# Older block's scores over the masked half: one turn for two blocks of attention weights

## The chip, the cores and the metric

The kernel runs on one core of a Trainium2 chip, so a run has one span. Time is device microseconds of that core; the runs of the kernel before took 629.08, 629.01 and 627.39 us, median 629.01. TensorE (PE) multiplies and turns matrices into PSUM; VectorE (DVE) and ScalarE (ACT) work on SBUF and PSUM; GpSimd (POOL) on SBUF; SyncE (SP) issues DMAs here. Engines run in order, each through its own list.

## The reference

Three layers follow each other: windowed attention with sinks, a gated product, and a mixture of experts with balanced routing. Only the attention is touched.

```python
batch, n_heads, seq, head_dim = (2, 8, 768, 64);  n_sink, window = (4, 128)
scores = (1 / sqrt(D)) * q @ k.T
keep = (pos[None, :] < n_sink) | ((rel >= 0) & (rel < window))     # rel = row - column
scores = where(keep, scores, -1e9);  a = exp(scores - max);  a /= sum(a) + 1e-9
return a @ v
```

A block of 128 queries sees its own block of 128 keys (lower triangle and diagonal), the older block before it (rel = 128 + row - column < 128: strictly the upper triangle), and the sinks. So for a window of up to 128 each pair of row and column is kept in at most one of the two blocks. Afterwards `x @ w_a * (x @ w_b) @ w_out` and the experts read the result.

## The kernel before

Attention is cut into 24 steps: 2 batches x 3 groups `g` of 256 queries (blocks `j` = 0, 1) x 4 pairs of heads `hp` (heads `h` = 0, 1). `attention` (L377) runs them as a software pipeline: iteration n (from -2 to 24) works on step n+2 (`turned`, L231), n+1 (`scores`, L257), n (`norm`: `factors`, `normed`, `sinks`; then `weights_turned` and `sinks_turned`) and n-1 (`copied`, `values`, `values_low`). The order of instructions on PE, ACT, DVE and POOL is the order of the code, written out by hand (`manual_schedule`, L595); SP's is planned.

In one iteration the order is: `norm` for step n, `copied` for n-1, `turned` for n+2, block 0's scores for n+1, `turned_low`, `values` and `values_low` for n-1, block 1's scores for n+1, then the turns of step n's weights and sinks. `fill` (L390) puts other PE work between them at seven places: dummy products up to iteration 8, and from iteration 9 on up to six products a time of the next stage (`early`, L460). From iteration 7 to 14 it also converts four raw weights (`word_steps`, L505: ACT, then DVE L518 to L525; the low part L541 on POOL), each over two iterations, the first of them the one that loads DVE (7, 9, 11, 13), the second POOL.

`scores` multiplies 128 queries with 264 columns for g > 0: the older block in columns 0 to 127, 8 sinks in 128 to 135, the own block in 136 to 263 (`KB` = 136). One DVE instruction (L277, shown as CUSTOM_DVE_ANT_0) adds the mask, scales, and keeps the row's extreme in `negmax`; ACT's exponential (L279) writes the weights `A2` and their `sums` (a second instruction reads the sum out). `factors` (L287, L288) makes 1/sum as `rs` on DVE; `normed` (L301) multiplies the weights by it on POOL, four instructions of 2 x 128 columns; `sinks` (L309 to L317) treats the sink columns on POOL. `weights_turned` (L334) turns up to 8 squares of 128 x 128 on PE: 2 blocks x 2 heads x (older, own). `copied` moves them to SBUF, head 0 on ACT (L349), head 1 on DVE (L347), the sinks on ACT (L343). `values` (L357, L367) multiplies with v.

Iterations 0 to 3 and 12 to 15 turn weights of g = 0 (no older block for block 0, so 6 squares, no sinks part); 4 to 11 and 16 to 23 have g > 0 and 8 squares. Scores run one iteration ahead: those of g > 0 stand in iterations 3 to 10 and 15 to 22.

PSUM has 8 buffers of 2 KB: 1 for turns of q and k, `SB` = 2 for scores, `ATB` = 3 for turned weights, 1 for values, 1 for the early products.

Of the kernel before, what the change touches and what calls it, by code (L numbers as in the profile page):

```python
# [9 lines left out]
F32 = mybir.dt.float32  # L10
F32R = mybir.dt.float32r
BF = mybir.dt.bfloat16
F16 = mybir.dt.float16
I32 = mybir.dt.int32
AF = mybir.ActivationFunctionType
# [35 lines left out]
         8: (("w", 3),), 9: (("v", 3), ("s", 1), ("q", 4), ("k", 4)), 13: (("v", 4), ("q", 5), ("k", 5)), 14: (("v", 5),)}  # L51
CONV_AT = (7, 9, 11, 13)
CONV_ON = (0, 0, 0, 0, 1)
SB, ATB = 2, 3
SINK = 8
WB, AB, NB, FB = 4, 2, 1, 2
KB = 128 + SINK
# [6 lines left out]
def f32(ap):  # L64
    return ap.bitcast(F32)


class Kernel:
# [17 lines left out]
    def constants(self, ctx, ge, att):  # L86
        nc, tc = self.nc, self.tc
        self.consts = c = ctx.enter_context(tc.tile_pool(name="consts", bufs=1))
        self.gep = ge.enter_context(tc.tile_pool(name="ge", bufs=1))
        m = att.enter_context(tc.tile_pool(name="masks", bufs=1))  # L90
        self.idle = m.tile([128, 512], BF, name="idle")
        nc.vector.memset(self.idle, 0.0)
        with tc.tile_pool(name="setup", bufs=1, side="right") as sp:
            rel = sp.tile([128, 128], F32, name="rel")
            nc.gpsimd.iota(rel, pattern=[[-1, 128]], base=0, channel_multiplier=1,
                           allow_small_or_imprecise_dtypes=True)
            self.ident = c.tile([128, 128], F32, name="ident")
            nc.vector.tensor_scalar(self.ident, rel, 0.0, None, op0=OP.is_equal)
            self.identr = m.tile([128, 128], F32R, name="identr")
            nc.vector.tensor_copy(self.identr, self.ident)  # L100
            raw = sp.tile([128, 2, 2], I32, name="raw")
            for i, s in enumerate((self.n_sink, self.window)):
                flat = bass.AP(tensor=s.tensor, offset=0, ap=[[1, 1]]).bitcast(I32)
                nc.gpsimd.dma_start(raw[:, i, :], bass.AP(tensor=flat.tensor, offset=0, ap=[[0, 128], [1, 2]]))
            col = sp.tile([128, 128], F32, name="col")
            nc.gpsimd.iota(col, pattern=[[1, 128]], base=0, channel_multiplier=0,
                           allow_small_or_imprecise_dtypes=True)
            low = sp.tile([128, 128], F32, name="low")
            nc.vector.tensor_scalar(low, rel, 0.0, None, op0=OP.is_ge)
            rel1 = sp.tile([128, 128], F32, name="rel1")  # L110
            nc.gpsimd.tensor_scalar(rel1, rel, 128.0, 1.0, op0=OP.add, op1=OP.mult)
            val = sp.tile([128, 2, 2], F32, name="val")
            nc.vector.tensor_copy(val, raw)
            neg = sp.tile([128, 2, 1], F32, name="neg")
            nc.vector.scalar_tensor_tensor(neg, val[:, :, 0:1], 0.0, val[:, :, 1:2], op0=OP.is_lt, op1=OP.add)
            sw = self.sw = c.tile([128, 2], F32, name="sw")
            nc.vector.scalar_tensor_tensor(sw, neg[:, :, 0], 4294967296.0, val[:, :, 0], op0=OP.mult, op1=OP.add)
            ns, win = sw[:, 0:1], sw[:, 1:2]

            def bias(eng, dst, keep):  # L120
                eng.tensor_scalar(dst, keep, BIG, -BIG, op0=OP.mult, op1=OP.add)

            snk = sp.tile([128, 128], F32, name="snk")
            nc.vector.tensor_scalar(snk, col, ns, None, op0=OP.is_lt)
            own = sp.tile([128, 128], F32, name="own")
            nc.vector.scalar_tensor_tensor(own, rel, win, low, op0=OP.is_lt, op1=OP.mult)
            own0 = sp.tile([128, 128], F32, name="own0")
            nc.vector.tensor_max(own0, own, snk)
            self.mask0 = m.tile([128, 128], F32, name="mask0")
            bias(nc.vector, self.mask0, own0)  # L130
            prev = sp.tile([128, 128], F32, name="prev")
            nc.vector.tensor_scalar(prev, rel1, win, None, op0=OP.is_lt)
            prev0 = sp.tile([128, 128], F32, name="prev0")
            nc.vector.tensor_max(prev0, prev, snk)
            self.mask1 = m.tile([128, 256 + SINK], F32, name="mask1")
            nc.gpsimd.memset(self.mask1[:, 128:KB], -BIG)
            bias(nc.gpsimd, self.mask1[:, KB:], own)
            bias(nc.gpsimd, self.mask1[:, 0:128], prev0)
            self.mask2 = m.tile([128, 256 + SINK], F32, name="mask2")
            bias(nc.gpsimd, self.mask2[:, 0:128], prev)  # L140
            bias(nc.gpsimd, self.mask2[:, 128:KB], snk[:, 0:SINK])
            bias(nc.gpsimd, self.mask2[:, KB:], own)
        self.negmax = c.tile([128, self.B * 6 * self.H], F32, name="negmax")
        self.sums = m.tile([128, self.B * 6 * self.H], F32, name="sums")

# [111 lines left out]
    def scores(self, st, j):  # L257
        nc, b, g, hp = self.nc, st.b, st.g, st.hp
        i = 2 * g + j
        if j == 0:  # L260
            st.A2 = self.aw.tile([128, 2, 2, 256 + SINK], F32, name="A", tag="A", bufs=4)
            st.r2 = self.aw.tile([128, 2, 2], F32, name="rs", tag="rs", bufs=4)
        T = self.T[b, hp]
        flat = T.rearrange("p t k c -> p t (k c)")
        c0 = KB if i == 0 else 0
        lo, n = (0, 128) if i == 0 else (KB * (i - 1), 256 + SINK)
        mask = self.mask0 if i == 0 else self.mask1 if i == 1 else self.mask2
        col0 = ((b * 6 + i) * self.H) + 2 * hp
        for h in range(2):
            s = self.atps.tile([128, 256 + SINK], F32, name="s", tag="s", bufs=SB)  # L270
            hs = slice(64 * h, 64 * h + 64)
            for t, (tq, tk) in enumerate(((0, 0), (0, 1), (1, 0))):
                nc.tensor.matmul(s[:, :n], T[hs, tq, 6 + i % 2, 0:128], flat[hs, tk, lo:lo + n],  # L273
                                 start=(t == 0), stop=(t == 2))
            sm = self.aw.tile([128, 256 + SINK], F32, name="sm", tag="sm", bufs=4)
            cc = slice(col0 + h, col0 + h + 1)
            nc.vector.tensor_tensor_reduce(out=sm[:, :n], in0=s[:, :n], in1=mask, scale=-self.scale, scalar=BIG,  # L277
                                           op0=OP.add, op1=OP.min, accum_out=self.negmax[:, cc])
            nc.scalar.activation(st.A2[:, j, h, c0:], sm[:, :n], AF.Exp, bias=self.negmax[:, cc], scale=-1.0,  # L279
                                 accum_out=self.sums[:, cc])  # L280

    def factors(self, st):
        nc = self.nc
# [6 lines left out]
    def normed(self, st):  # L290

        nc = self.nc
        i0 = 2 * st.g
        for h in range(2):
            for j in range(2):
                A = st.A2[:, j]
                blocks = A[:, h, KB if i0 + j == 0 else 0:]
                if i0 + j > 1:
                    blocks = bass.AP(tensor=A.tensor, offset=A.offset + h * (256 + SINK),
                                     ap=[list(A.ap[0]), [KB, 2], [1, 128]])  # L300
                nc.gpsimd.tensor_scalar(blocks, blocks, st.r2[:, j, h:h + 1], 1.0, op0=OP.mult, op1=OP.mult)  # L301

    def sinks(self, st):
# [15 lines left out]
    def sinks_turned(self, st):  # L319
# [3 lines left out]
        pt = self.atps.tile([128, 2, 128], F32R, name="pt", tag="at", bufs=ATB)  # L323
        for n in range(2):
            nc.tensor.transpose(pt[:, n, :], st.AS[:, n], self.identr)
        st.ps.append((pt[0:6 * SINK], None))

    def weights_turned(self, st, h):
        nc = self.nc
        pa = self.atps.tile([128, 4, 128], F32, name="pa", tag="at", bufs=ATB)  # L330
        a0 = 0 if st.g else 1
        for a in range(a0, 4):
            cols = slice(0, 128) if a % 2 == 0 else slice(KB, KB + 128)
            nc.tensor.transpose(pa[:, a, :], st.A2[:, a // 2, h, cols], self.ident)  # L334
        st.ps.append((pa, a0))

    def copied(self, st):

        nc = self.nc
        for n, (pa, a0) in enumerate(st.ps):  # L340
            if n == 2:
                st.ast = self.aw.tile([6 * SINK, 2, 128], F32R, name="ast", tag="ast", bufs=2)
                nc.scalar.activation(st.ast, f32(pa), AF.Copy)  # L343
                continue
            at = self.aw.tile([128, 4, 128], F32, name="at", tag="atb", bufs=4)
            if n:
                nc.vector.tensor_copy(at[:, a0:], pa[:, a0:])  # L347
            else:
                nc.scalar.activation(at[:, a0:], pa[:, a0:], AF.Copy)  # L349
            st.AT.append(at)  # L350

    def values(self, st):
        nc, D, b, g, hp = self.nc, self.D, st.b, st.g, st.hp
# [1000 lines left out]
```

## Time and profile before

| | |
|---|---|
| median of 3 runs | 629.01 us (627.39 to 629.08) |
| profiled execution | 627.7 us, of which the span 625.6 us |
| busy over the span | PE 97%, DVE 64%, ACT 54%, POOL 29% |
| granted TensorE clock | 0.9 or more of full speed in all but the last of 40 slices, 0.996 in the mean |
| attention | about 4.8 us to 130 us of the span |
| turned weights (L334) | 176 squares, 272 ns one in the median, 26.4 us of PE together |
| ScalarE's table loads | one, at the start; Exp, Copy, Abs, Sign and Relu all run later |

Busy time counts an instruction from start to end; matmuls overlap, so a busy PE can still have gaps between starts. In a time line a row's first number is its start, the second the time to its end. The first turn of q and k of an iteration (L237) tells where it begins: iteration 4 at 27.0 us, 6 at 35.7, 7 at 40.1, 9 at 50.2, 12 at 67.0, 16 at 86.5, 19 at 102.5, 20 at 107.9.

### The profile page before, as it was taken

What the parts mean: (1) busy time and instruction counts of PE and PEld (TensorE: products, weight loads), DVE (VectorE), ACT (ScalarE), POOL (GpSimd) and SP (SyncE); (2) the same over time, 40 slices, a digit from 0 to 9 for tenths busy, and PEclk for the clock granted to TensorE, in tenths of its full rate; (3) what the DMA queues carried; (4) which work ended last, traced back from release to release, by engine and by line L of the source; (5) the groups of instructions that cost most, each with busy time, mean ns of one, the idle gap of its engine ahead of it and who ended that gap; (6) DMA issues with size and microseconds to landing.
All of it is one profiled execution on the core that took longest, in us unless ns stands there. A gap on an engine that the chain in (4) does not pass through costs nothing.

```text
span 625.6 us, 10135 instructions
## 1 busy us (share of the span) xinstructions
PE 608.3 (97%) x3645; PEld 477.0 (76%) x3645; DVE 403.3 (64%) x864; ACT 339.0 (54%) x672; POOL 178.5 (29%) x300
## 2 busy tenths in 40 slices
PE   7999999999999999999999999999999999999994
PEld 5667777778877887777867766777788898888882
DVE  6788876669985766442114566656436878778781
ACT  4888777634552434213125566664436766667660
POOL 5657565410000000001024443434441322122221
PEclk9999999999999999999999999999999999999998
DMA  7977320025451433200031000000087788877841
GB/s 159 211 151 163 68 69 2 2 74 170 162 156 47 134 101 104 67 1 0 1 100 52 18 36 18 17 18 35 35 273 234 253 272 260 262 240 226 268 130 30
DMA packets 82602, 72.16 MB, mean 115 GB/s; under 512 B 41072, under 2 KB 69744, under 8 KB 82544
## 3 DMA queue, kind: packets, MB, share of 16 engines
q1 hardware_dynamic: 78704, 61.99, 34.0%
q0 software_dynamic: 2112, 6.30, 3.2%
q10 hardware_dynamic: 1728, 3.15, 1.3%
q8 instruction: 31, 0.51, 0.3%
q14 instruction: 27, 0.22, 0.1%
HBM read 65.13 MB, written 6.29 MB: 114 GB/s over the span
## 4 chain that ended last, share of the span: by engine, by line
PE 81%; issue 9%; POOL 2%; DVE 2%; DMA 2%; ACT 2%; SPq 0%; POOLq 0%; DVEq 0%; ACTq 0%
PE pb L559 14%; PE px L995 14%; PE pa L559 14%; PE p L1110 7%; PE pa L470 4%; PE px L367 4%; PE s L273 4%; PE pa L334 3%; PE pq L874 2%; POOL out_dram L1125 2%; PE y L1116 1%; PE y L1117 1%; PE pt L237 1%; PE y L1121 1%; PE y L1118 1%
## 5 line engine op out<-in xcount | busy, mean ns | idle before, releaser
L1025 DVE TENSOR_TENSOR elo<-eraw,ehi 128x1024 fp32r<-128x1024 f32 x64 | 75.9, 1217 | 6.9 <-ACT ehi L1020 6.9
L1110 PE MATMUL p<-xt,ehi 128*128 128x384 f32 x256 | 73.2, 359 | 0.1
L981 POOL TENSOR_TENSOR gl<-G,gh 128x512 fp32r<-128x512 f32 (+1 forms) x40 | 48.7, 1225 | 66.2 <-ACT gh L980 62.3
L1020 ACT ACTIVATE ehi<-eraw 128x1024 fp32r<-128x1024 f32 x64 | 65.0, 1054 | 1.4 <-DMA eraw<-in_moe_w_dram 1.0
L1110 PE MATMUL p<-xt,elo 128*128 128x192 f32 x256 | 64.0, 251 | 0.0
L995 PE MATMUL px<-woh,gh 128*128 128x512 f32 x144 | 59.5, 413 | 0.0
L981 POOL TENSOR_TENSOR gl<-GE,gh 128x256 fp32r<-128x256 f32 x8 | 7.1, 883 | 182.0 <-ACT gh L980 178.5
L279 ACT ACTIVATE A<-sm,negmax 128x264 f32<-128x264 f32 (+1 forms) x96 | 46.9, 489 | 22.4 <-DVE negmax L277 21.3
L863 DVE TENSOR_SCALAR gt<-lgT,vmax 128x1536 bf16<-128x1536 f32 x40 | 45.5, 1199 | 20.1 <-ACT lgT L838 17.7
L995 PE MATMUL px<-woh,gl 128*128 128x512 f32 x144 | 57.2, 397 | 0.0
L995 PE MATMUL px<-wol,gh 128*128 128x512 f32 x144 | 57.0, 396 | 0.0
L301 POOL TENSOR_SCALAR A<-A,rs 128x256 f32<-128x256 f32 (+1 forms) x96 | 43.2, 468 | 43.4 <-DVE rs L288 23.9
L566 DVE TENSOR_TENSOR G<-asb,pb 128x512 f32<-128x512 f32 x32 | 21.9, 685 | 47.1 <-PE pb L559 47.0
L1125 POOL DMA_INDIRECT out_dram<-o,oidx x16 | 26.3, 1646 | 90.1 <-ACT o L1134 68.1
L559 PE MATMUL pb<-xh,whi 128*128 128x512 f32 x128 | 51.7, 404 | 0.0
L559 PE MATMUL pb<-xh,wlo 128*128 128x512 f32 x128 | 50.1, 392 | 0.0
L559 PE MATMUL pa<-xh,wlo 128*128 128x512 f32 x128 | 50.0, 390 | 0.0
L559 PE MATMUL pb<-xl,whi 128*128 128x512 f32 x128 | 49.9, 390 | 0.0
L559 PE MATMUL pa<-xl,whi 128*128 128x512 f32 x128 | 49.9, 390 | 0.0
L559 PE MATMUL pa<-xh,whi 128*128 128x512 f32 x128 | 49.8, 389 | 0.0
L1110 PEld LDWEIGHTS p<-xt,elo 128*128 128x128 f32 x256 | 48.8, 191 | 0.6 <-ACT xt L1087 0.3
L1110 PEld LDWEIGHTS p<-xt,ehi 128*128 128x128 f32 x256 | 48.0, 188 | 0.9 <-DVE xt L1088 0.3
(224 smaller groups left out, 1416.3 us busy)
## 6 DMA issues: line engine op xcount, KB each, us to landing
eraw<-in_moe_w_dram SPq DMA_DIRECT2D x64, 512.0 KB
wraw<-in_moe_w_a_dram SPq DMA_DIRECT2D x12, 512.0 KB
wraw<-in_moe_w_b_dram SPq DMA_DIRECT2D x12, 512.0 KB
wraw<-in_moe_w_out_dram SPq DMA_DIRECT2D x12, 512.0 KB
x2d<-x ACTq DMA_DIRECT2D x11, 256.0 KB
rawv<-in_v_dram SPq DMA_DIRECT2D x10, 256.0 KB
rawq<-in_q_dram SPq DMA_DIRECT2D x8, 256.0 KB
rawk<-in_k_dram SPq DMA_DIRECT2D x8, 256.0 KB
```

What stands on the lines that cost most here:

```text
L273: nc.tensor.matmul(s[:, :n], T[hs, tq, 6 + i % 2, 0:128], flat[hs, tk, lo:lo + n], start=(t == 0), stop=(t == 2))
L279: nc.scalar.activation(st.A2[:, j, h, c0:], sm[:, :n], AF.Exp, bias=self.negmax[:, cc], scale=-1.0, accum_out=self.sums[:, cc])
L301: nc.gpsimd.tensor_scalar(blocks, blocks, st.r2[:, j, h:h + 1], 1.0, op0=OP.mult, op1=OP.mult)
L367: nc.tensor.matmul(px[64 * h:64 * h + 64, cols], vv[:, vcol[h]], st.AT[h][:, sl].rearrange("p a b -> p (a b)"), start=(not g and n == 0), ...
L559: nc.tensor.matmul(pab[m], w[:, k, :], x[:, k, :], start=(k == 0 and t == 0), stop=(k == 3 and t == 2))
L863: nc.vector.tensor_scalar(gt, vrow, v, None, op0=OP.is_lt)
L981: nc.gpsimd.tensor_tensor(gl[:, fs], src, f32(gh[:, fs]), op=OP.subtract)
L995: nc.tensor.matmul(out[t], w[:, ff, :], x[f], start=(f == 0 and n == 0), stop=(f == 11 and n == 2))
L1020: self.nc.scalar.activation(hi, raw, AF.Copy)
L1025: (eng or self.nc.vector).tensor_tensor(lo, raw, f32(hi), op=OP.subtract)
L1110: nc.tensor.matmul(p1[:, ff, 0:c], w[:, k, cols], x[:, k, 0:c], start=(n == 0), stop=(k == 3), skip_group_check=True)
L1125: st = nc.gpsimd.indirect_dma_start(out=self.out, out_offset=bass.IndirectOffsetOnAxis(ap=self.oidx[:n, 2 * e + h:2 * e + h + 1], axis=0), ...
```

## The change

For g > 0 the scores of the older block are copied in PSUM over the own block's columns where the own block is masked (above the diagonal). Mask, maximum, exponential and sum then run on 136 columns (sinks, merged square) instead of 264. POOL multiplies the merged square by +1 on and below the diagonal and -1 above it; normalising and turning handle one square for both blocks. After the turn, ACT's Relu takes the positive part (own block) and DVE takes the negated part clipped at zero (older block), both into one SBUF tile. Buffers for scores become 3, for turned weights 2. For g = 0 the instructions stay, with one tile for both heads.

```diff
-SB, ATB = 2, 3
+SB, ATB = 3, 2
@@ constants
-            self.mask2 = m.tile([128, 256 + SINK], F32, name="mask2")
-            bias(nc.gpsimd, self.mask2[:, 0:128], prev)
-            bias(nc.gpsimd, self.mask2[:, 128:KB], snk[:, 0:SINK])
-            bias(nc.gpsimd, self.mask2[:, KB:], own)
+            self.mask2 = m.tile([128, KB], F32, name="mask2")
+            bias(nc.gpsimd, self.mask2[:, 0:SINK], snk[:, 0:SINK])
+            both = sp.tile([128, 128], F32, name="both")
+            nc.vector.tensor_max(both, own, prev)
+            bias(nc.gpsimd, self.mask2[:, SINK:], both)
+            self.older = m.tile([128, 128], I32, name="older")
+            nc.vector.tensor_scalar(self.older, rel, 0.0, None, op0=OP.is_lt)
+            self.sign = m.tile([128, 128], F32, name="sign")
+            nc.vector.tensor_scalar(self.sign, low, 2.0, -1.0, op0=OP.mult, op1=OP.add)
@@ scores
+        m0 = 128 if g else 0
...
-            nc.vector.tensor_tensor_reduce(out=sm[:, :n], in0=s[:, :n], in1=mask, scale=-self.scale, scalar=BIG,
+            if g:
+                nc.vector.copy_predicated(s[:, KB:], self.older, s[:, 0:128])
+            nc.vector.tensor_tensor_reduce(out=sm[:, m0:n], in0=s[:, m0:n], in1=mask, scale=-self.scale, scalar=BIG,
                                            op0=OP.add, op1=OP.min, accum_out=self.negmax[:, cc])
-            nc.scalar.activation(st.A2[:, j, h, c0:], sm[:, :n], AF.Exp, bias=self.negmax[:, cc], scale=-1.0,
+            nc.scalar.activation(st.A2[:, j, h, c0 + m0:], sm[:, m0:n], AF.Exp, bias=self.negmax[:, cc], scale=-1.0,
                                  accum_out=self.sums[:, cc])
+        if g:
+            block = st.A2[:, j, :, KB:]
+            nc.gpsimd.tensor_tensor(block, block, self.sign.unsqueeze(1).to_broadcast([128, 2, 128]), op=OP.mult)
@@ normed
-                blocks = A[:, h, KB if i0 + j == 0 else 0:]
-                if i0 + j > 1:
-                    blocks = bass.AP(tensor=A.tensor, offset=A.offset + h * (256 + SINK),
-                                     ap=[list(A.ap[0]), [KB, 2], [1, 128]])
+                blocks = A[:, h, KB if j == 0 or st.g else 0:]
@@ weights_turned
+        if st.g:
+            if h == 0:
+                st.ps.append(self.atps.tile([128, 2, 2, 128], F32, name="pa", tag="at", bufs=ATB))
+            for j in range(2):
+                nc.tensor.transpose(st.ps[0][:, h, j, :], st.A2[:, j, h, KB:], self.ident)
+            return
...
@@ copied
+        if st.g:
+            pa, ps = st.ps
+            at = self.aw.tile([128, 2, 2, 2, 128], F32, name="at", tag="atb", bufs=2)
+            nc.scalar.activation(at[:, :, :, 1], pa, AF.Relu)
+            nc.vector.tensor_scalar(at[:, :, :, 0], pa, -1.0, 0.0, op0=OP.mult, op1=OP.max)
+            st.ast = self.aw.tile([6 * SINK, 2, 128], F32R, name="ast", tag="ast", bufs=2)
+            nc.scalar.activation(st.ast, f32(ps), AF.Copy)
+            st.AT = [at[:, h].rearrange("p j o b -> p (j o) b") for h in range(2)]
+            return
...
```

## Rows read from the trace of the kernel before

**Rows 1.** Stretches: from:to us, busy us (instructions) of PE, PEld, DVE, ACT, POOL; clock, DMA, GB/s.
```profile
27.00:40.10 13.10, 12.63 (x114) 9.29 (x113) 10.26 (x42) 11.07 (x37) 7.83 (x24) 1.00 1.14 242
40.10:67.00 26.90, 25.28 (x215) 19.05 (x214) 23.77 (x78) 21.76 (x69) 19.52 (x47) 1.00 0.50 111
...
86.50:130.70 44.20, 44.20 (x356) 33.37 (x355) 29.04 (x103) 29.89 (x91) 21.69 (x66) 1.00 0.03 9
```
**Rows 2.** Time line of ACT, iteration 6: start, us, engine, line, out<-in, count [idle].
```profile
35.76 0.50 ACT L279 ACTIVATE A<-sm,negmax 128x264 f32<-128x264 f32 x1
36.16 0.18 ACT L279 ACTIVATION_READ_ACCUMULATOR A<-sm,negmax 128x1 f32 x1
...
39.62 0.52 ACT L279 ACTIVATE A<-sm,negmax 128x264 f32<-128x264 f32 x1 [0.40 <-DVE negmax L277]
```
**Rows 3.** Time line of DVE, iteration 6 and the start of 7.
```profile
36.45 0.17 DVE L287 TENSOR_SCALAR rs<-sums 128x4 f32<-128x4 f32 x1 [0.56 <-ACT A L279]
36.66 0.18 DVE L288 RECIPROCAL rs<-rs 128x4 f32<-128x4 f32 x1
36.75 0.66 DVE L347 COPY at<-pa 128x512 f32<-128x512 f32 x1
...
39.15 0.43 DVE L277 CUSTOM_DVE_ANT_0 sm<-s,mask 128x264 f32<-128x264 f32 x1 [0.43 <-PE s L273]
...
39.51 0.43 DVE L277 CUSTOM_DVE_ANT_0 sm<-s,mask 128x264 f32<-128x264 f32 x1
...
40.84 0.17 DVE L287 TENSOR_SCALAR rs<-sums 128x4 f32<-128x4 f32 x1 [0.55 <-ACT A L279]
```
**Rows 4.** Time line of PE, iteration 6.
```profile
37.46 1.09 PE L367 MATMUL px<-at,rawv 128*64 128x256 f32 x12
38.48 0.64 PE L273 MATMUL s<-T 64*128 64x264 f32 x6
```
**Rows 5.** Time line of POOL, iteration 6.
```profile
37.03 1.84 POOL L301 TENSOR_SCALAR A<-A,rs 128x256 f32<-128x256 f32 x4 [1.70 <-PE s L273]
38.84 0.24 POOL L309 TENSOR_TENSOR asf<-A,rs 128x32 f32<-128x32 f32 x1
...
39.45 0.25 POOL L317 TENSOR_TENSOR AS<-asf,AS 128x32 fp32r<-128x32 f32 x1
```
**Rows 6.** Time line of PE, iterations 19 and 20.
```profile
104.15 1.09 PE L367 MATMUL px<-at,rawv 128*64 128x256 f32 x12
106.07 0.60 PE L334 MATMUL pa<-ident,A 128*128 128x128 f32 x4
...
109.53 0.65 PE L367 MATMUL px<-at,rawv 128*64 128x256 f32 x4
```
**Rows 7.** Groups by shape: line, engine, out<-in, count | busy us, mean ns | idle before.
```profile
L277 DVE CUSTOM_DVE_ANT_0 sm<-s,mask 128x128 f32<-128x128 f32 x16 | 3.9, 283 | 2.0 <-PE s L273 2.0
L279 ACT ACTIVATE A<-sm,negmax 128x128 f32<-128x128 f32 x16 | 6.3, 395 | 1.9 <-DVE negmax L277 1.9
L301 POOL TENSOR_SCALAR A<-A,rs 128x128 f32<-128x128 f32 x16 | 6.0, 372 | 11.2 <-DVE rs L288 3.4 <-PE s L273 2.8 <-DVE negmax L277 2.0
```
**Rows 8.** One line's instructions: count, ns of the shortest, median, longest; starts; shape.
```profile
L981 POOL TENSOR_TENSOR gl<-GE,gh x8: 728/738/1456, 290.9 to 401.3; 128x256 fp32r<-128x256 f32 x8
```
**Rows 9.** Time lines of DVE and POOL at the heads of iterations 9 and 11.
```profile
50.91 0.57 DVE L287 TENSOR_SCALAR rs<-sums 128x4 f32<-128x4 f32 x1 [0.56 <-ACT A L279]
50.94 0.52 POOL L203 MEMSET vraw<- 48x512 f32 x1
...
60.48 1.28 POOL L541 TENSOR_TENSOR wlo<-wf,whi 128x512 fp32r<-128x512 f32 x1
61.36 0.43 DVE L287 TENSOR_SCALAR rs<-sums 128x4 f32<-128x4 f32 x1 [0.56 <-ACT A L279]
```
**Rows 10.** Time lines of DVE and POOL at 11 us.
```profile
10.78 0.69 DVE L252 TENSOR_TENSOR T<-pt,T 128x512 fp32r<-128x512 f32 x1
11.53 0.22 POOL L255 CAST T<-T 128x40 fp32r<-128x40 f32 x1 [1.07 <-DVE T L252]
```

More of the change, by code (lines that the diff above doesn't have):

```diff
@@ L325, in sinks_turned @@
             nc.tensor.transpose(pt[:, n, :], st.AS[:, n], self.identr)
-        st.ps.append((pt[0:6 * SINK], None))
+        st.ps.append(pt[0:6 * SINK])
     def weights_turned(self, st, h):
         nc = self.nc
+        if st.g:
[4 more added lines that the diff above has]
+            return
         pa = self.atps.tile([128, 4, 128], F32, name="pa", tag="at", bufs=ATB)
-        a0 = 0 if st.g else 1
-        for a in range(a0, 4):
+        for a in range(1, 4):
             cols = slice(0, 128) if a % 2 == 0 else slice(KB, KB + 128)
             nc.tensor.transpose(pa[:, a, :], st.A2[:, a // 2, h, cols], self.ident)
-        st.ps.append((pa, a0))
+        st.ps.append(pa)
     def copied(self, st):
         nc = self.nc
[L340 to L350, printed above, removed]
+        if st.g:
[7 more added lines that the diff above has]
+            return
+        at = self.aw.tile([128, 2, 4, 128], F32, name="at", tag="atb", bufs=2)
+        nc.scalar.activation(at[:, 0, 1:], st.ps[0][:, 1:], AF.Copy)
+        nc.vector.tensor_copy(at[:, 1, 1:], st.ps[1][:, 1:])
+        st.AT = [at[:, h] for h in range(2)]
     def values(self, st):
```

## The prediction

> **What bounds the kernel now.** I read the table by stretches first, then the time lines of two iterations, then the groups by shape. The change touches only the attention, 24 steps run by the software pipeline of iterations -2 to 24. In iterations 4 to 6 no engine is full: 13.1 us hold 10.3 us of VectorE and 11.1 us of ScalarE, 4.37 us an iteration [rows 1]. What binds there is a loop through four engines, followed here from one end of the second exponential's sum (T, 36.16 + 0.18 = 36.34) to the next [rows 2 to 4]. `rs` starts at 36.45 and its reciprocal at 36.66; VectorE's copy of the turned weights runs from 36.75 to 37.41; TensorE's value products start at 37.46 and block 1's scores at 38.48; the first mask-and-maximum starts at 39.15, the first exponential at 39.62, and the next `rs` at 40.84. That closes 4.39 us, the whole iteration. In iterations 7 to 11 VectorE also converts weights: 23.8 of 26.9 us [rows 1], so there its queue sets the pace. From iteration 16 on TensorE also carries products of the next stage and is busy throughout [rows 1]; the value products follow each other at 104.15 and 109.53, every 5.38 us [rows 6]. After 130.7 us TensorE stays full, so what the attention gains or loses goes into the total one for one.
>
> **The change part by part.** With g > 0, four of eight turns of weights go in each of 16 iterations (4 to 11, 16 to 23). Four turns in a row take 0.60 us [rows 6] and one alone 0.27 (the profile's table), so each further one costs (0.60 - 0.27)/3 = 0.11 us: 0.44 us an iteration, 7.0 us in all. Where the loop or VectorE binds, this is worth nothing; where TensorE binds, it takes 5.38 to 4.94, if nothing else comes late there.
>
> The copy over the masked half is new: one on VectorE for each head and block, in the loop ahead of each mask-and-maximum. No row has this operation. Below, it can't be shorter than the tiniest VectorE step here, 0.17 us for 4 columns [rows 3]; above, I bound it by the mask-and-maximum of 264 columns, 0.43 us [rows 3]. I take the one of 128 columns, 0.28 us [rows 7], which also reads PSUM and one tile of SBUF. Call it c. A dependent VectorE step starts 0.04 after its forerunner's end (36.62 to 36.66), an independent one 0.07 before it (39.58 and 39.51) [rows 3]. So the second head's mask-and-maximum starts at c + 0.04 + 0.22 + c + 0.03 = 2c + 0.29 after block 1's scores; it takes 0.29 for 136 columns, the exponential follows 0.05 later, lasts 0.40 instead of 0.50 [rows 2, 7] and its sum ends 0.08 after it: about 2c + 1.12. Before, the same stretch took 40.84 - 0.11 - 39.15 = 1.58. The difference is 2c - 0.46: +0.10 us at c = 0.28, and -0.12 to +0.40 at the ends. [...]
>
> The multiplication by sign is new on POOL, two an iteration, 128 x 256. POOL's TENSOR_TENSOR of that shape takes 0.74 us where it runs alone, up to 1.46 beside VectorE [rows 8]. POOL has room: its four factors of 128 columns shrink from 0.46 to 0.35 each [rows 5, 7], and 0.86 us of sink work follow (38.84 to 39.70) [rows 5]. In sum 1.4 + 0.9 + 1.5 = 3.8 us an iteration, under the loop. The cost lies elsewhere. The sign of block 1 is released by the same event as VectorE's `rs`, at T. POOL starts 0.06 us after what releases it when it waits for one engine (11.47 to 11.53) [rows 10], `rs` 0.11 after [rows 2, 3]. So POOL is likely in first, and VectorE's small TENSOR_SCALAR does not end while POOL is at work: at 61.36 it took 0.43 us and ended at 61.79, with POOL's TENSOR_TENSOR at 61.76; at 50.91 it took 0.57 and ended at 51.48, with POOL's MEMSET at 51.46 [rows 9]. [...] Were `rs` first, its price would be none; that is the first rival.) `rs` then ends at T + 0.06 + 0.74 + 0.03 = T + 0.83 instead of T + 0.28: +0.55 us, with the reciprocal, the copy and the values all queued behind it. The new loop is 4.39 + 0.10 + 0.55 = 5.03 us.
>
> The other edits I cost at nothing: ScalarE's Relu and VectorE's negative part have the 512 columns of the two copies they replace, 0.66 us on VectorE [rows 3], with Relu in the table set loaded once at the start; the sum of sinks still ends before TensorE turns it; the wider tile makes ScalarE wait for all turns, which end 0.4 us earlier now. Three PSUM buffers for scores let block 1's first head not wait for the slower mask steps; two for turned weights match the two tiles now used. The three new constants (some 0.8 us of VectorE at 0.28 each) fall in the wait for the first scores; 0.5 us if that cover fails.
>
> The sum, by iterations:
> - 3: its scores get the copies: +0.1.
> - 4 to 6: 3 x 5.03 - 13.1 = +2.0.
> - 7: VectorE's queue is full, so the copies count at both blocks: at block 0 twice (0.28 + 0.04 + 0.22 - 0.36), which is 0.36, at block 1 the loop's 0.10; `rs` waits as well: +1.0.
> - 8: +0.10 + 0.55 = +0.65.
> - 9: here POOL is full. In 8 it starts its factors at T + 1.24 and ends them at 2.68, the sinks at 3.54, sign 0 at 4.28, a weight's low part (1.28 us [rows 9]) at 5.56, sign 1 at 6.30, and the MEMSET of 0.52 [rows 9] at 6.82. `rs` ends 1.82 us after its T (6.85 - 5.03) instead of 0.68 (51.48 - 50.91 + 0.11): +1.14, and +0.46 for the copies: +1.6.
> - 10, with 11's `rs`: the same stack without MEMSET, while TensorE gives back 0.44: +0.2. 11: 0.
> - 12 to 15 are g = 0 and don't change.
> - 16 to 21: the period falls from 5.38 to the larger of 4.94 (TensorE) and 5.03 (loop): five times -0.35, and about half of that in 16, where the pace sets in: -1.9. 22 and 23, without turns of q and k, are not TensorE's: +0.3.
>
> Total +0.1 + 2.0 + 1.0 + 0.65 + 1.6 + 0.2 - 1.9 + 0.3 = +3.9 us. The profiled execution took 627.7 us (span 625.6), which makes 631.6; the median of the runs, 629.0, is 1.3 above it, so the forecast is 632.9 us. By c alone (0.17 to 0.43) it moves from 630.6 to 637.4, as the loop can't push iterations 16 to 21 under TensorE's 4.94.
>
> **The rivals.**
> - `rs` goes first (20%). For it: the margin is 0.05 us, and an extra wait on POOL's sign would turn it (POOL started its first factor 0.19 after the reciprocal, where it waited for more than one engine [rows 3, 5]). Against it: the sign needs ScalarE alone. The loop is 4.48, so 4 to 6 cost +0.3 and 7 +0.46. POOL's stack still holds `rs` in 9 (+1.3) and 11 (+0.5). Iterations 16 to 21 get TensorE's 0.44 six times, and 22, 23 another 0.6: -3.2. Together -0.6: 628.4 us.
> - Faster (15%): TensorE gets its turns back in full because the copy is cheap. Place: ahead of block 1's mask. Price: c of 0.17, with `rs` not held. Then the loop is 4.26: -0.3 in 4 to 6, nothing in 7, +0.9 in 9, +0.3 in 10 and 11, -3.2 later: -2.3, 626.7 us. It decides once c + half of what holds `rs` is under some 0.25 us. For it: the copy does no arithmetic; against it: no VectorE row that reads 128 columns of PSUM is under 0.28.
> - POOL becomes the bound (7%): if a sign takes the 1.46 us of the contended rows [rows 8], `rs` is held 0.72 longer in some 15 iterations: +11, 644 us. Against it: VectorE reads PSUM at that time, and POOL's factors keep their 0.46 beside it [rows 5].
>
> **How the numbers follow.** The forecast has 58%. A difference under 0.3% (1.9 us) can't be told from none here. Faster by more than that: the second rival, and 5% from tails of the others: 0.20. Within it: most of the first rival and the low end of the forecast: 0.21. Slower: 0.59. Range 626.5 to 638.5: down to the faster rival, up past the dear copy; what is left out is mostly POOL as the bound.
>
> **What would show it.** `rs` (TENSOR_SCALAR, 0.17 us now) would read about 0.7 us in nearly every iteration with g > 0 and end with POOL's multiplication. Iterations 4 to 6 would take about 5.0 us, 17 to 21 also about 5.0, with TensorE's idle time now before the value products. The copy would read 0.28 us. The prediction is wrong if `rs` keeps 0.17, if iterations 17 to 21 reach 4.94 while 4 to 6 stay at 4.4, or if anything after the attention moves by more than 1 us.

## The result and the profile after

The changed kernel takes 637.7 us (median of 4 runs, 635.81 to 638.46), the kernel before 629.05 beside it (4 runs, 627.39 to 629.33): a ratio of 1.0139, 95% interval 1.0117 to 1.0162, so 8.7 us slower. The forecast was 632.9, 3.9 us slower. The profiled execution took 636.94 us, its span 634.9, 9.3 more than before.

All of that lies in the attention: its last value product ends 9.4 us later than before (138.94 for 129.51 us), and behind it nothing moved by more than 0.2 us. The table counts from the start of one iteration's `rs` to the start of the next one's, summed over stretches, in the profiled executions; the forecast's column is its own sum.

| iterations | before, us | after, us | difference | forecast |
|---|---|---|---|---|
| 3 | 4.03 | 4.26 | +0.23 | +0.1 |
| 4 to 6 | 12.79 | 15.33 | +2.54 | +2.0 |
| 7 to 11 | 26.47 | 33.25 | +6.78 | +3.45 |
| 12 to 15 | 19.14 | 19.39 | +0.25 | 0 |
| 16 to 22 (the forecast with 23) | 36.77 | 36.62 | -0.15 | -1.6 |

The sum is +9.65; iterations 0 to 2 and what lies at both ends take 0.2 off it, hence 9.4.

The stretches that answer to [rows 1], with the same columns:

```profile
27.00:40.10 13.10, 9.67 (x83) 6.43 (x83) 11.70 (x45) 8.75 (x31) 9.04 (x26) 1.00 1.21 243
40.10:67.00 26.90, 21.40 (x157) 15.81 (x153) 23.78 (x78) 16.41 (x53) 18.05 (x43) 0.81 0.46 111
86.50:130.70 44.20, 42.83 (x336) 30.74 (x335) 38.33 (x147) 30.96 (x106) 32.65 (x81) 1.00 0.08 25
```

In the last stretch VectorE works 38.3 us where it worked 29.0, POOL 32.7 for 21.7, and TensorE, which was never idle there, has 1.4 us of gaps. In the middle one VectorE is as full as before, and the granted clock is 0.81 instead of 1.00. By finer stretches it is at half speed, 0.50 to 0.51, three times, each time after a stretch in which TensorE stood idle for a good part (2.20 of 3.50 us busy from 37.0 to 40.5, then 4.80 of 6.90, then 7.64 of 10.30):

```profile
40.50:43.90 3.40, 3.40 (x21) 2.75 (x19) 2.63 (x11) 2.48 (x11) 1.97 (x6) 0.51 0.32 72
43.90:50.80 6.90, 4.80 (x41) 3.48 (x41) 6.69 (x22) 3.91 (x14) 4.17 (x11) 0.99 0.13 35
50.80:57.60 6.80, 6.05 (x33) 4.49 (x35) 5.00 (x18) 4.38 (x15) 5.25 (x13) 0.50 0.47 119
57.60:67.90 10.30, 7.64 (x67) 5.44 (x65) 9.94 (x32) 6.14 (x20) 7.10 (x20) 1.00 0.67 160
67.90:71.30 3.40, 3.40 (x13) 2.67 (x14) 2.95 (x11) 2.09 (x7) 3.40 (x8) 0.50 0.00 0
```

The time line of iteration 5, which answers to [rows 3 to 5], then pieces of 7, 8, 9, 11, 17 and of 19 and 20:

```profile
32.80 0.72 POOL L293 TENSOR_TENSOR A<-A,sign 128x256 f32<-128x256 f32 x1 [0.74 <-ACT A L288]
32.83 0.72 DVE L300 TENSOR_SCALAR rs<-sums 128x4 f32<-128x4 f32 x1 [0.30 <-ACT A L288]
...
33.59 0.18 DVE L301 RECIPROCAL rs<-rs 128x4 f32<-128x4 f32 x1
33.68 0.66 DVE L359 TENSOR_SCALAR at<-pa 128x512 f32<-128x512 f32 x1
33.94 1.41 POOL L311 TENSOR_SCALAR A<-A,rs 128x128 f32<-128x128 f32 x4 [0.41 <-DVE rs L301]
34.26 0.28 DVE L285 COPY_PREDICATED s<-older,s 128x128 f32<-128x128 int32 x1
...
34.40 1.09 PE L384 MATMUL px<-at,rawv 128*64 128x256 f32 x12 [0.49 <-DVE at L359]
34.58 0.30 DVE L286 CUSTOM_DVE_ANT_0 sm<-s,mask 128x136 f32<-128x136 f32 x1
...
37.88 0.73 POOL L293 TENSOR_TENSOR A<-A,sign 128x256 f32<-128x256 f32 x1 [1.01 <-ACT A L288]
37.91 0.72 DVE L300 TENSOR_SCALAR rs<-sums 128x4 f32<-128x4 f32 x1 [0.30 <-ACT A L288]
...
46.81 0.69 DVE L537 SCALAR_TENSOR_TENSOR wf<-wraw,wf 128x512 int32<-128x512 int32 x1
46.91 1.17 POOL L293 TENSOR_TENSOR A<-A,sign 128x256 f32<-128x256 f32 x1
...
47.54 1.10 DVE L539 SCALAR_TENSOR_TENSOR wf<-wraw,wf 128x512 int32<-128x512 int32 x1
...
52.12 1.97 PE L384 MATMUL px<-at,rawv 128*64 128x256 f32 x12 [0.48 <-DVE at L359]
54.02 1.03 PE L280 MATMUL s<-T 64*128 64x264 f32 x6
...
56.89 0.73 POOL L293 TENSOR_TENSOR A<-A,sign 128x256 f32<-128x256 f32 x1 [1.07 <-ACT A L288]
56.92 1.18 DVE L300 TENSOR_SCALAR rs<-sums 128x4 f32<-128x4 f32 x1 [0.30 <-ACT A L288]
...
72.61 0.29 DVE L286 CUSTOM_DVE_ANT_0 sm<-s,mask 128x128 f32<-128x128 f32 x1 [1.09 <-PE s L280]
...
101.91 0.17 DVE L300 TENSOR_SCALAR rs<-sums 128x4 f32<-128x4 f32 x1 [0.23 <-ACT A L288]
101.95 0.73 POOL L293 TENSOR_TENSOR A<-A,sign 128x256 f32<-128x256 f32 x1 [0.79 <-ACT A L288]
...
108.27 1.09 PE L384 MATMUL px<-at,rawv 128*64 128x256 f32 x12
...
113.36 1.09 PE L384 MATMUL px<-at,rawv 128*64 128x256 f32 x12
```

`rs` takes 0.72 us, where it took 0.17, and ends 0.03 after POOL's multiplication, to the row as forecast; `rs` to `rs` is 5.08 us, forecast 5.03. What the forecast does not have are the last pieces. In iteration 7 block 0's sign and VectorE's conversions get in each other's way (1.17 us for 0.72, 1.10 for 0.69). In 8 the value products take 1.97 us for 1.09 and the score products behind them 1.03 for 0.64, at half the clock. In 11 VectorE waits 1.09 us for scores, as TensorE comes out of the third slow stretch (to 71.3) late. And late the period is 113.36 - 108.27 = 5.09 us, against 5.38 in [rows 6].

The groups by shape that answer to [rows 7]:

```profile
L293 POOL TENSOR_TENSOR A<-A,sign 128x256 f32<-128x256 f32 x32 | 25.1, 784 | 18.9 <-ACT A L288 18.9
L286 DVE CUSTOM_DVE_ANT_0 sm<-s,mask 128x136 f32<-128x136 f32 x64 | 19.1, 298 | 2.1
L285 DVE COPY_PREDICATED s<-older,s 128x128 f32<-128x128 int32 x64 | 18.5, 289 | 3.3 <-PE s L280 3.1
```

The copy costs 289 ns, as taken. 64 of them are 18.5 us of VectorE.

### The profile page after: what moved, and what is told of

It is laid out like the page before. It is cut to its first block, busy times and chain, and to the rows that moved or that the text cites. A ratio compares the mean times of both kernels' runs of the same rounds, so it can differ in the third digit from the quotient of the medians.

```text
span 634.9 us, 10096 instructions
## 1 busy us (share of the span) xinstructions
PE 609.6 (96%) x3581; PEld 474.9 (75%) x3581; DVE 421.1 (66%) x931; ACT 335.1 (53%) x672; POOL 193.5 (30%) x331
## 4 chain that ended last, share of the span: by engine, by line
PE 75%; issue 10%; DVE 8%; POOL 2%; DMA 2%; ACT 2%; SPq 0%; POOLq 0%; DVEq 0%; ACTq 0%
PE pb L576 14%; PE px L1012 14%; PE pa L576 14%; PE p L1127 7%; PE px L384 3%; PE pa L487 3%; PE s L280 2%; PE pq L891 2%; POOL out_dram L1142 2%; DVE rs L300 2%; DVE sm L286 1%; PE y L1133 1%; PE y L1134 1%; PE y L1138 1%; PE y L1135 1%
## 5 line engine op out<-in xcount | busy, mean ns | idle before, releaser
L288 ACT ACTIVATE A<-sm,negmax 128x136 f32<-128x136 f32 (+2 forms) x96 | 40.5, 423 | 35.7 <-DVE negmax L286 29.8
L582 ACT ACTIVATE asb<-pa 128x512 f32<-128x512 f32 x32 | 19.0, 593 | 52.0 <-PE pa L576 51.9
```

Of the source, the lines that this page charges most:

```text
L288: nc.scalar.activation(st.A2[:, j, h, c0 + m0:], sm[:, m0:n], AF.Exp, bias=self.negmax[:, cc], scale=-1.0, accum_out=self.sums[:, cc])
```

## The experiments

Fourteen kernels ran. Ratios are to the kernel before in the same session, with 95% intervals; the other columns are the stretches of the first table, in us, from one profile each. The texts set apart were written before each run.

| kernel | ratio | 4 to 6 | 7 to 11 | 16 to 22 |
|---|---|---|---|---|
| before | 1 | 12.79 | 26.47 | 36.77 |
| after | 1.0139 (1.0117 to 1.0162) | 15.33 | 33.25 | 36.62 |
| e3_ones | 1.0057 (1.0037 to 1.0076) | 14.45 | 29.77 | 37.26 |
| e4_nosign | 1.0015 (1.0001 to 1.0029) | 13.59 | 27.86 | 35.41 |
| e2_later | 1.0067 (1.0043 to 1.0091) | 13.60 | 29.03 | 36.36 |
| e6_nocopy | 0.9991 (0.9972 to 1.0009) | 13.44 | 27.29 | 34.76 |
| e9_copies | 1.0199 (1.0172 to 1.0225) | 14.96 | 29.50 | 40.84 |
| e10_neither | 0.9882 (0.9855 to 0.9909) | 12.04 | 24.75 | 33.77 |
| e1_keep | 1.0128 (1.0101 to 1.0155) | 14.96 | 32.20 | 36.60 |
| e5_keep2 | 1.0130 (1.0104 to 1.0157) | 15.23 | 31.50 | 36.64 |
| e14_block1 | 1.0116 (1.0094 to 1.0138) | 14.97 | 31.27 | 36.80 |
| e7_sb2 | 1.0181 (1.0155 to 1.0208) | 14.98 | 32.25 | 38.40 |
| e8_hybrid | 1.0019 (1.0004 to 1.0033) | 12.78 | 26.50 | 37.72 |
| e11_subtract | 0.9984 (0.9970 to 0.9998) | 13.09 | 27.81 | 34.30 |
| e12_apart | 0.9996 (0.9979 to 1.0012) | 13.09 | 28.59 | 34.33 |
| e13_half | 0.9973 (0.9959 to 0.9987) | 12.78 | 26.48 | 34.56 |

**The hold.** The kernel before, with POOL's two multiplications an iteration put in, by ones (e3_ones):

```diff
+        if g:
+            block = st.A2[:, j, :, KB:]
+            nc.gpsimd.tensor_tensor(block, block, self.ones.unsqueeze(1).to_broadcast([128, 2, 128]), op=OP.mult)
```

> The kernel before, with nothing of the change but POOL's multiplication, here by ones, on the own block of the weights (same size, same place). Theory 1: rs reads about 0.72 us in most iterations with g > 0, iterations 4 to 6 take 4.9 us instead of 4.4, iterations 17 to 21 keep 5.4, and the time is 1.006 to 1.013 of the kernel before (the upper end if the clock falls as well). Theory 2: under 1.003, since POOL has room.

Every `rs` of iterations 4 to 7 takes 0.72 or 0.73 us and the loop 4.94 instead of 4.38: +0.56, the forecast's 0.55. So the multiplications alone, with nothing else of the change, cost 0.57%, just under what theory 1 gave. They cost little from iteration 16 on, where TensorE's 5.38 covers 4.94.

The kernel after without the multiplication (e4_nosign; all weights then go to the own block's values):

```diff
-        if g:
-            block = st.A2[:, j, :, KB:]
-            nc.gpsimd.tensor_tensor(block, block, self.sign..., op=OP.mult)
```

> The changed kernel without the multiplication by sign; it leaves out the telling apart of the two blocks, so older weights stay with the own block's keys. All else runs as in the changed kernel. Theory 1: loop of 4.5 us in iterations 4 to 6, 4.9 to 5.0 in 17 to 21, clock at or near 1.00, and 0.993 to 1.000 of the kernel before. Theory 2: above 1.006, since the copies on VectorE remain.

```profile
33.59 0.58 ACT L354 ACTIVATE at<-pa 128x512 f32<-128x512 f32 x1
33.79 0.17 DVE L296 TENSOR_SCALAR rs<-sums 128x4 f32<-128x4 f32 x1 [0.30 <-ACT A L288]
33.99 0.18 DVE L297 RECIPROCAL rs<-rs 128x4 f32<-128x4 f32 x1
...
34.20 0.69 DVE L355 TENSOR_SCALAR at<-pa 128x512 f32<-128x512 f32 x1
```

1.24% of the time goes, less than expected, to a ratio between the two theories: the loop falls to 4.67 us, not to the first rival's 4.48. The time line shows one reason. The negative part starts 0.21 us behind the reciprocal's start, 0.09 in the kernel after: it waits for a semaphore that ScalarE raises, and ScalarE's Relu of the same squares ends only at 34.17. In the kernel after `rs` comes so late that this wait is covered: in iteration 5 Relu ends at 33.20, the negative part starts at 33.68.

The same multiplication moved out of the way (e2_later): block 1's stands behind POOL's first two factors, which wait for `rs`.

```diff
-        if g:
+        if g and j == 0:
...
+        for j in range(2):
+            if st.g and j == 1:
+                (block 1's multiplication)
+            for h in range(2):
```

> The changed kernel, with block 1's multiplication by sign moved on POOL from right after the exponentials to behind the first two factors, that is behind rs. Same instructions, another order. Theory 1 (POOL holds rs for 0.55 us an iteration, and the gaps that this leaves cost the clock): rs reads 0.17 us again, iterations 4 to 6 take about 4.5 us, the clock stays nearer 1.00 in 40 to 70 us, and the time is 0.997 to 1.003 of the kernel before. Theory 2 (the copies on VectorE and its conversions are the cost, not the hold): rs reads 0.17, but the time stays above 1.008.

The ratio falls from 1.0139 to 1.0067, between the two theories. `rs` is back at 0.17 us nearly everywhere and the loop at 4.67, with all of POOL's work still there: in the loop it was the order on POOL, not the amount. The amount costs elsewhere, as the ratio stays 0.52% above that without the multiplications: in iteration 9 `rs` is still held, 1.52 us, by the low part of a weight and a MEMSET, and 9 takes 7.62 us for 6.52, 16 takes 6.83 for 5.89.

**The copies.** The kernel after without them (e6_nocopy):

```diff
-            if g:
-                nc.vector.copy_predicated(s[:, KB:], self.older, s[:, 0:128])
```

> The changed kernel without the copies of the older block's scores; it leaves the older block out of the weights. Masks, exponentials, signs and turns run as in the changed kernel. Theory 1 (each copy costs its 0.29 us and two gaps in the loop, about 0.5 us an iteration, and double where VectorE's queue is full): rs to rs is 4.5 to 4.7 us in iterations 4 to 6 (5.1 with copies), 1.003 to 1.007 of the kernel before. Rival (the copies hide, the hold by POOL is all): 5.0 us, 1.011 or more.

The ratio is 0.9991, below what either theory gave: the copies are worth 1.5%, 9.3 us, within the change. With the hold in place (`rs` 0.73) the loop is 4.60 us instead of 5.08, as theory 1 had it, and from iteration 18 to 21 the period is 4.92 to 5.01, about the forecast's 4.94 for TensorE with half the turns.

The other way round, the kernel before with the copies alone (e9_copies):

```diff
+            if g:
+                nc.vector.copy_predicated(s[:, KB:], self.older, s[:, 0:128])
             nc.vector.tensor_tensor_reduce(out=sm[:, :n], in0=s[:, :n], in1=mask, ...
```

> The kernel before, and in it only the copies of the older block's scores over the masked half of the own block, ahead of each mask-and-maximum with g > 0; nothing else is changed (the mask still covers both blocks, so the result is that of before). Theory 1: a copy costs VectorE's whole queue its 0.28 us and a dependent gap of 0.04 at each of two heads, 0.64 us wherever VectorE's chain or queue sets the pace, and nothing where TensorE does. Iterations 4 to 6 then take 5.0 us instead of 4.39, iterations 7 and 9 get 1.0 to 1.3 us longer, 16 to 21 keep 5.38 apart from 0.6 in 15 or 16: ratio 1.009 to 1.013. Theory 2: the copies are dear only together with the sign and the merged square (without them the kernel took 9.3 us less); alone they find room in VectorE's waits, iterations 4 to 6 stay under 4.7 and the ratio under 1.006.

1.0199 is 12.5 us, well over what theory 1 gave. Where VectorE sets the pace it was right: 4 to 6 take 4.90 to 5.03 each, 7 gets 1.23 longer, 9 a little less than said, 0.82. The rest lies where it saw nothing: iterations 16 to 22 take 4.1 us more, 19 to 21 some 5.85 each for 5.38, though TensorE has the pace there. The rows of one such iteration:

```profile
109.41 0.30 DVE L280 COPY_PREDICATED s<-older,s 128x128 f32<-128x128 int32 x1 [0.79 <-PE s L275]
109.74 0.43 DVE L281 CUSTOM_DVE_ANT_0 sm<-s,mask 128x264 f32<-128x264 f32 x1
110.10 0.08 DVE L281 DVE_READ_ACCUMULATOR2_ANT negmax<- 128x1 f32 x1
110.10 0.29 DVE L280 COPY_PREDICATED s<-older,s 128x128 f32<-128x128 int32 x1
110.42 0.43 DVE L281 CUSTOM_DVE_ANT_0 sm<-s,mask 128x264 f32<-128x264 f32 x1
...
110.44 1.10 PE L275 MATMUL s<-T 64*128 64x264 f32 x6
```

Block 1's six score products take 1.10 us instead of 0.64 [rows 4]: with two score buffers the second head's three wait until VectorE has masked block 0's second head. The two copies make that 0.64 later, and TensorE stands for 0.46 of it, about 5.85 - 5.38. The copies alone on three buffers were not run.

Neither copies nor sign, that is what the change saves by itself (e10_neither):

> The kernel after without the copies and without the sign: the older block is left out of the weights, and the work that is left is what the change saves. Theory 1: the two costs share one queue and don't add: without the copies 9.3 us went, without the sign 7.8, and without both some 11 to 13, because TensorE then holds iterations 17 to 21 at 4.94 and the conversions hold 7 to 11; iterations 4 to 6 take 4.0 to 4.2; ratio 0.992 to 0.997. Theory 2: they add, 17 us, ratio 0.986 to 0.990.

0.9882, as theory 2 had it: 7.4 us are saved, and the two costs all but add. From there the copies cost 1.33% (without the sign), the sign 1.09% (without the copies). The three sum to +1.24%; the whole change is at +1.39%, which is not further off than the intervals reach. So the change is a saving of 7 us that two prices of 8 and 7 us bury.

**The lowered clock.** The kernel after with dummy products, of no use to the result, put into TensorE's waits: eight ahead of the values of iterations 7 to 12 (e1_keep); then in iterations 4 to 11, there and behind the sinks' product, and ahead of block 1's scores in 7 and 9 (e5_keep2; in this second kernel they take the place of part of that bank's sums, which are left out):

```diff
+        for _ in range(KEEP.get((b, g, hp), 0)):
+            nc.tensor.matmul(px[:, 256:512], self.idle[:, 0:128], self.idle[:, 0:256], start=True, stop=True, ...
```

> The changed kernel, with eight dummy products (128 x 256, into unused columns of the value bank) ahead of the value products of iterations 7 to 12, where TensorE waits and its granted clock falls to half. Theory 1 (the clock): of the 9 us that the change cost, the 4 to 5 beyond the forecast are TensorE's products at half speed in iterations 7 to 11. Then the clock reads 1.00 there, iterations 8 and 10 shrink from 8.9 and 8.5 us to about 6, and the time falls from 1.014 to about 1.006 to 1.008 of the kernel before. Theory 2 (the queues): VectorE's conversions and POOL's stack hold the loop anyway and the low clock is only their shadow. Then the clock rises too, but the time stays at 1.012 or more.

> The changed kernel with dummy products wherever TensorE waits in iterations 4 to 11: eight ahead of the value products, four behind the sinks' product, eight ahead of block 1's scores in iterations 7 and 9. Six iterations of such dummies left one stretch of half clock (52 to 59 us) of the three that the changed kernel showed (41 to 44, 51 to 58, 68 to 71). Theory 1 (the half clock costs 2 to 3 us of the 9): clock 1.00 from 20 us on, iteration 8 at 5.1 from rs to rs instead of 6.3, 1.007 to 1.011 of the kernel before. Theory 2 (low clock costs nothing, since TensorE waits anyway): clock 1.00, but the time at 1.013 to 1.015.

The first kept only part: the clock was still low from 52.1 to 58.9 us (0.85 in the mean from 54 to 70), and iteration 12, one of those with dummies, took 6.08 us for 4.56, so nothing follows from its ratio. The second held it:

```profile
27.00:40.50 13.50, 13.50 (x118) 9.73 (x118) 11.92 (x47) 8.85 (x30) 9.25 (x25) 1.00 1.13 240
40.50:71.30 30.80, 30.49 (x260) 22.17 (x256) 27.78 (x96) 21.24 (x69) 23.89 (x57) 1.00 0.45 94
```

Iteration 8 falls from 6.33 to 5.05 us, the forecast's loop, and the rows say by what: value and score products are back at 1.09 and 0.63. But 10 grows by 1.0, and there the dummies (`px<-idle`) are in the way:

```profile
52.37 1.09 PE L392 MATMUL px<-at,rawv 128*64 128x256 f32 x12
53.39 0.63 PE L281 MATMUL s<-T 64*128 64x264 f32 x6
...
63.41 0.66 DVE L360 TENSOR_SCALAR at<-pa 128x512 f32<-128x512 f32 x1
64.62 0.61 PE L382 MATMUL px<-idle 128*128 128x256 bf16 x4
65.16 1.09 PE L392 MATMUL px<-at,rawv 128*64 128x256 f32 x12
66.84 0.30 DVE L286 COPY_PREDICATED s<-older,s 128x128 f32<-128x128 int32 x1 [1.07 <-PE s L281]
```

The squares for the values are there at 64.07, but TensorE works on dummies until 65.16, and VectorE then waits 1.07 us for the scores. 7 to 11 together fall by 1.75 and the attention ends 1.1 us earlier; the ratio, 1.0130 against 1.0139, is where theory 2 had it and doesn't tell the difference from nothing. So the run shows what the low clock costs in iteration 8. What it costs the kernel in all stays open, as the dummies take back part of what they give.

**Block 0's sign.** The kernel after with block 1's sign alone (e14_block1):

```diff
-        if g:
+        if g and j == 1:
```

> The kernel after with the sign of block 1 alone; block 0's is left out, so for block 0 both blocks' weights go to the own block's values. Theory 1: block 0's sign is not free, it holds VectorE's conversions in 7 and 9 (which then read 0.7 us again) and pushes POOL's stack: iterations 7 to 11 take 31 to 32.5 us instead of 33.25, 4 to 6 the same 15.3 as after; ratio 1.009 to 1.012. Theory 2: it lies beside other work and costs nothing, as the forecast had it: ratio 1.013 to 1.015, 7 to 11 within 0.5 us of 33.25.

7 to 11 take 31.27 us, 1.98 less, as theory 1 had it, and the conversion is back:

```profile
46.16 0.68 DVE L537 SCALAR_TENSOR_TENSOR wf<-wraw,wf 128x512 int32<-128x512 int32 x1
46.88 0.69 DVE L539 SCALAR_TENSOR_TENSOR wf<-wraw,wf 128x512 int32<-128x512 int32 x1
```

7 and 9 get 0.42 and 0.44 shorter, as much as their conversions. That is the sign's price, 0.86 us. The rest of the 1.98 is not: 11 gets 1.13 shorter, but the clock no longer falls there, and in two kernels that keep block 0's sign and whose clock is at 1.00 there, 11 takes about as little (5.86 us in e1_keep, 5.88 in e7_sb2, 5.79 here). The ratio, 1.0116, can't be told from 1.0139: the intervals overlap.

**The buffers.** The kernel after with the numbers of before (e7_sb2):

```diff
-SB, ATB = 3, 2
+SB, ATB = 2, 3
```

> The changed kernel with the PSUM buffers of the kernel before: two for scores, three for turned weights. If the third buffer for scores buys something under the longer mask steps: 1.015 to 1.020 of the kernel before, with TensorE waiting for the masks ahead of block 1's scores. If it doesn't matter, as the forecast has it: 1.012 to 1.016.

1.0181: by the medians the third score buffer saves 0.42%, 2.6 us, though the two intervals just overlap. In the profile 1.8 us of it lie from 16 on (38.40 for 36.62), where the run with the copies alone showed what two buffers cost.

**Towards a better kernel.** First the change in the second batch alone, where TensorE sets the pace, with block 1's sign behind the factors, two score buffers, and the kernel before in the first batch (e8_hybrid):

```diff
+            m0 = 128 if b and g else 0
+            if m0:
+                mask = self.mask3
+                nc.vector.copy_predicated(s[:, KB:], self.older, s[:, 0:128])
```

> A version meant to be faster than both: the merged square only for the second batch (scores in iterations 15 to 22), where TensorE is the bound, with block 1's sign behind rs; the first batch as before. From the rows of the run with the later sign: iterations 17 to 21 at 4.9 instead of 5.4 us, 15 and 16 longer by 0.5 in all, so 0.996 to 1.000 of the kernel before. If the turns that go are not TensorE's bound, 1.000 to 1.003.

1.0019, slower than meant. The first batch is as before, but 16 to 22 take 37.72 us for 36.77, 18 to 21 some 5.2 each; that this is the copies on two buffers again is read from the run before, not tested here. The copies have to go, and the mask isn't the only place to merge the blocks. After the exponential each square holds zeros where the other has weights, so own minus older is the merged, signed square in one instruction on POOL, the price of the sign alone (0.73 us; e11_subtract, then e12_apart):

```diff
-        m0 = 128 if g else 0
+        m0 = 0
...
-                nc.vector.copy_predicated(s[:, KB:], self.older, s[:, 0:128])
...
-            nc.gpsimd.tensor_tensor(block, block, self.sign..., op=OP.mult)
+            nc.gpsimd.tensor_tensor(block, block, st.A2[:, j, :, 0:128], op=OP.subtract)
```

> The merged square in another way: masks and exponentials over 264 columns as before the change, and POOL subtracts the older block's weights from the own block's (one instruction of 128 x 256 in the place of the sign), block 1's behind block 0's factors, so behind rs. No copy and no multiplication by sign; turns, Relu, negative part and buffers as in the kernel after. Theory 1: copies and hold were the whole cost; iterations 4 to 6 take 4.4 to 4.65 (the negative part still waits for Relu), 17 to 21 take 4.94, rs 0.17 us in most iterations: ratio 0.996 to 1.001. Theory 2: POOL's longer stack (two subtractions ahead of the turns) sets the pace in 7 to 11 and delays the turns: ratio 1.002 to 1.007.

> As the version with the subtraction, and the tile that Relu and the negative part write is laid out in two halves of its own instead of interleaved squares, so that VectorE need not wait for ScalarE. Theory 1: the negative part starts with the reciprocal's end, some 0.2 us earlier where the loop binds (4 to 6, 8, 10, 22): 1.0 to 1.5 us less than the version before it, ratio 0.994 to 0.999. Theory 2: the wait stands for something else (the PSUM bank that both read) and stays: the same ratio as the version before it.

The subtraction gives 0.9984 (0.9970 to 0.9998), as theory 1 had it: 4.93 us in 18 to 21, a loop of 4.53, but 1.3 us lost in 7 to 11: iteration 8 takes 5.84 us for the loop's 4.53, with the clock at half from 47.5 to 54.4 (value products of 1.98 us there). Laying the tile out in halves changes nothing that can be told; the negative part still starts only as Relu ends (36.68 and 36.65 us), so the interleaving was not its cause: theory 2.

```profile
36.08 0.57 ACT L353 ACTIVATE at<-pa 128x512 f32<-128x512 f32 x1
36.68 0.69 DVE L354 TENSOR_SCALAR at<-pa 128x512 f32<-128x512 f32 x1
```

The traces say that it is a wait which the program holds: the negative part waits for a semaphore that ScalarE raises (in the kernel after an idle stretch of 0.9 us ahead of it ends with Relu), where VectorE's copy in the kernel before waits for one that TensorE raises (0.7 us, ended by the turns). Why the program has that wait, for the PSUM bank that both read or for another reason, was not tried.

Last, the subtraction in the second batch alone, the first as before (e13_half):

> The kernel before for the first batch (iterations up to 11), the subtraction on POOL in the place of copies and sign for the second (weights of 16 to 23): turns, Relu and negative part as in the kernel after there, masks, exponentials and the numbers of PSUM buffers as before. Theory 1: iterations 3 to 14 keep their times of before, 16 to 22 take 4.93 with 15 and 16 as before, some 34.3 to 35 us instead of 36.8: ratio 0.996 to 0.998, less than either kernel. Theory 2: with two score buffers TensorE waits for VectorE's masks there as in the run with copies alone, and 16 to 22 stay at 36 to 37: ratio 0.999 to 1.002.

```profile
104.81 1.09 PE L397 MATMUL px<-at,rawv 128*64 128x256 f32 x12
...
109.73 1.09 PE L397 MATMUL px<-at,rawv 128*64 128x256 f32 x12
```

The value products follow each other 4.92 us apart instead of 5.38, iterations 3 to 15 take what they took before, and the ratio is 0.9973 (0.9959 to 0.9987). This beats both kernels, by 0.3% of the one before; two score buffers are enough without the copies.

## Why the forecast had the sign right and the size wrong

- **What binds** was read rightly in 4 to 11, the loop and then VectorE's queue, and nothing behind the attention moved by more than 0.2 us. TensorE's period from 16 on was read from two iterations only (below).
- **The hold** was right in place, cause and size: 0.72 us for `rs`, +0.56 in the loop (e3_ones), gone from the loop with the order on POOL (e2_later). VectorE's small step ends just behind POOL's instruction in the trace, 37.91 + 0.72 = 38.63 behind 37.88 + 0.73 = 38.61; by what the two engines hold each other no run shows.
- **The copy** was sized rightly, 0.289 us for 0.28. In iterations 4 to 6 the sum came out nearly as well, +2.54 for +2.0. Iteration 6 has 0.36 more by the clock (5.44 us; 5.08 with the clock at full in e14_block1), and the 13.1 that was taken off should have been 12.79, `rs` to `rs`; iteration 4, at 4.81 under the loop, makes up for 0.2 of it.
- **The step that failed is the sum over 7 to 11: +3.45 forecast, +6.78 measured.** By iteration, forecast and measured: 7 +1.0 and +1.55, 8 +0.65 and +1.95, 9 +1.6 and +1.64, 10 +0.2 and +0.67, 11 none and +0.98. Two things were missing in it.
  - **TensorE's clock.** The sum has TensorE's products at full speed. The change leaves TensorE idle for a good part there (21.40 of 26.90 us busy, 25.28 before), and its granted clock fell to 0.50 in stretches. Iteration 8, forecast at the loop's 5.03, took 6.33: 0.88 more for the value products and 0.39 more for the scores behind them. With the clock kept it took 5.05 (e5_keep2). In 11 VectorE waits 1.09 us for late scores; where the clock was at 1.00 there, it took 5.86 and 5.88 (e1_keep, e7_sb2), as good as the 5.94 of before. Together that is some 2.3 of the 3.3 us that are missing.
  - **Block 0's sign.** It was costed at nothing because "POOL has room". POOL has, but VectorE hasn't: that sign runs beside conversions that work on SBUF, and each holds the other, 0.42 us in 7 and 0.44 in 9 (e14_block1).
  - That 9 came out was luck: its `rs` was to end 1.82 us after T and ended 1.28 after it (58.10; T was 56.82), as POOL was idle for 1.07 us ahead of block 1's sign (56.89), iteration 8 having lasted longer. In 10 the loop held, 5.05, where the forecast let TensorE give back 0.44.
  - These are readings of one profile for each kernel. In the ratios neither part can be told from noise, and what the clock costs the kernel in all stays open.
- **16 to 23: -1.6 forecast, -0.15 measured.** The loop was right there too (5.09 for 5.03 in 19 and 20), but the saving was taken "five times" from a period of 5.38 that [rows 6] show for 19 and 20. Iterations 16 and 17 took 5.70 and 4.52 before, 5.11 in the mean, so against the loop's 5.03 there was next to nothing to save; they take 5.92 and 5.13 now. That is 1.3 us of the 1.45 that are missing. TensorE's saving is real, 4.92 and 4.93 us in 19 and 20 where copies or sign are left out (e6_nocopy, e4_nosign).
- **15** was left out of the sum: it carries the scores of step 16 and so four copies, +0.46, as 3 does, which was counted.
- **The buffers** were costed at nothing. The third score buffer is worth some 2.6 us within this change; without it the forecast's error would have been larger. **Relu and the negative part** were costed at nothing too; the negative part waits for Relu, which the hold covers in the kernel after and which shows without it (loop 4.67 for the first rival's 4.48).
- **The rivals.** `rs` went first in two of the sixteen iterations with g > 0 alone, 17 and 18, and read 0.17 us there (101.91, POOL's sign behind it at 101.95), as the first rival had it; it read 0.69 to 0.74 in twelve, 1.18 in 9 and 0.53 in 11. The copy was not cheap, and POOL was not the bound for the signs that hold `rs`. Three of block 0's signs took 1.17 to 1.19 us, that rival's case of a sign made longer beside VectorE, but they cost VectorE's queue, if anything, and not `rs`.

## What to carry to other kernels

Price a new step on an idle engine by what the other engines do at that moment, not by its own idle time: here two instructions of 0.73 us an iteration on an engine with 30% of load cost 7 to 8 us, and moving one of the two behind the step that everybody waits for gave back more than half. An engine that the change relieves can slow down (TensorE, 4.80 of 6.90 us busy, then had half the clock for 6.8 us), so what it still does in the loop may cost more than before (value products of 1.97 us for 1.09). Read a period from all of the iterations that it is to be multiplied with. And when two operands are zero where the other isn't, merge them where an idle engine can, not in the queue of the one that is late.

## What the runs showed of the hardware beside that

- A predicated copy of 128 x 128 in PSUM took 289 ns of VectorE in the mean of 64, and moved what follows by 0.32 us (34.26 to 34.58).
- VectorE and POOL lengthened each other on SBUF in iteration 7: a conversion of 0.69 us took 1.10 and the POOL instruction beside it 1.17 for 0.73.
- The granted clock fell to half (0.50 to 0.51) in three stretches of 3.4 to 6.8 us of the changed kernel; with TensorE kept busy for 30.49 of 30.80 us it stayed at 1.00. Where it fell the value products took 1.97 us for 1.09. Keeping it up with dummy products moved the end of the attention by 1.1 us only, as the dummies held up iteration 10 by 1.0.
